# The second MoE product of six token blocks by seven quarter products instead of eight, on one core

## The chip, the cores and the metric

The kernel runs on one core of a Trainium2 chip. The metric is the device time of one launch in microseconds, the median of several runs. A profile of one execution shows what each engine did in it: PE is TensorE (PEld its weight loads), DVE is VectorE, ACT is ScalarE, POOL is GpSimd and SP is SyncE, which issues the DMAs.

## The reference

Retention attention of 8 batches with 8 heads, 576 positions and 64 dimensions, then a gated feed-forward product over all 4608 tokens:

```
scores = scale * q @ k.T                     # per batch and head, 576 x 576
Dmat = gamma_h ** (row - col) where row >= col, else 0
x = (scores * Dmat) @ v                      # heads side by side: 4608 x 512
h = x @ w_in                                 # 512 x 2048
g = h * (1 / (1 + exp(-beta * h)))           # beta per hidden column
out = g @ w_out                              # 2048 x 512, float32
```

## The kernel before

The decay is split into gains for queries and values (`gq`, `gv`), so that attention is linear: the 512 first positions of a batch are worked in chunks, with masked scores inside a chunk (`scores`, L510) and running states between chunks (`fold`, L492), and `outputs4` (L543) adds both parts and leaves `xT`, 512 tokens with the hidden index on the partitions. The last 64 positions of all batches make one more block of 512 tokens (`tail_scores`, `tail_outputs`). There are nine blocks, in the order batch 0 to 6, tails, batch 7.

A block has two products. `up` (L630) is one step of 4 matmuls of 512 columns, for one of 16 groups `fo` of 128 hidden columns; ScalarE's silu (L639) writes the result to `gT`. `down` (L663) makes the output for 128 tokens at a time from 16 matmuls of 512 columns, in steps of 4; `gT` is the stationary side, `w_out_sb` the moving one. The factor 1/beta is in `w_out_sb` (`cast_w_out`, L211), since silu(beta h) is beta times g. VectorE copies each finished `po` to `ot` (L677), and SP stores it.

The order of all engines' instructions is written out by hand. `fill` lists the steps of the products, and `base[n]` is the step at which block n begins. The streams hold pairs of a step number and a piece of other work; `merged` (L690) puts each piece before the step of that number. So one step is 4 matmuls of 512 columns, and a block of 32 steps is followed by the next with no gap. In blocks 2 to 5 the attention of the next batch stands at step 16 (scores and second states) and step 25 or 26 (`outputs4`), in the second product. Loads, the gains on GpSimd (`pre_q` L281, `pre` L318 and L292) and the DMA transposes `x_q`, `x_k` stand a fixed number of steps ahead of the scores that use them (`pair_prep`).

Each engine works its own instructions in that order, and waits by semaphores. Places that the prediction speaks of:

- PSUM tiles take banks by tag: `mm` (3 banks, for `ph`, `po` and the second state bank), `O` (2), `sc` (2), `st` (1). A new tile of a tag waits until the work on the tile whose bank it takes is done.
- `four_states` leaves four state updates in two banks. `fold` adds them one after another in float32 (VectorE, L499, alternately into `sums` and `warm`), and ScalarE copies each sum to a bf16 tile in `sbq` (L503).
[...]
- `load_w_out` brings the four groups of `w_out` in float32 to tiles `wt`, of which there are four.

Of the kernel before, what the change touches and what calls it, by code (L numbers as in the profile page):

```python
# [19 lines left out]
def kernel(  # L20
# [15 lines left out]
    P = 128  # L36
# [11 lines left out]

    blocks = list(range(B - 1)) + [B, B - 1]

    seq = []
# [120 lines left out]
    w_in_sb = wpool.tile([P, KO, d_ff], BF16, name="w_in_sb")  # L172
    w_out_sb = wpool.tile([P, FO, d_model], BF16, name="w_out_sb")
    beta_sb = consts.tile([P, FO], F32, name="beta_sb")
    rbeta_sb = consts.tile([P, FO], F32, name="rbeta_sb")
    tiny = consts.tile([P, FO], F32, name="tiny")
    WG = 4

# [32 lines left out]
    def cast_w_out(g):  # L211
        t = wts.pop(NP + g)
        for i in range(KO):
            fo = g * KO + i
            if g and i == KO - 1:
                nc.scalar.activation(w_out_sb[:, fo, :], t[:, i], ACT.Copy, scale=rbeta_sb[:, fo:fo + 1])
            else:
                nc.vector.tensor_scalar(w_out_sb[:, fo, :], t[:, i], rbeta_sb[:, fo:fo + 1], None, ALU.mult)

    for g in range(NP):  # L220
# [23 lines left out]
    def xt(m):  # L244
        if m not in xts:
            xts[m] = xpool.tile([P, HP, CB, P], BF16, name="xT", tag="xT" if m < B else "xTt", bufs=2 if m < B else 1)
        return xts[m]

    def F(f, *a):
        return lambda: f(*a)  # L250
# [17 lines left out]
    def pre_q(b, n):  # L268

        if n == 0:  # L270
            batch[b] = dict(qs=sb.tile([P, CB, H, D], BF16, name="qs", tag="qs", bufs=2),
                            qT=sb.tile([P, CB, HP, P], BF16, name="qT", tag="qT", bufs=2))
        if b < 2:
            hs, cs = slice(n // 2 * HP, (n // 2 + 1) * HP), slice(n % 2 * 2, n % 2 * 2 + 2)
            e = nc.vector
        else:
            if n % 2:
                return
            cs = slice(n, n + 2)
            for to, hs in turned:  # L280
                nc.gpsimd.tensor_tensor(batch[b]["qs"][:, cs, to], q_tiles[b][:, hs, cs].rearrange("p h i d -> p i h d"),  # L281
                                        gq[:, cs, hs].unsqueeze(3).to_broadcast([P, 2, len(range(H)[hs]), D]), ALU.mult)
            return
        e.tensor_tensor(batch[b]["qs"][:, cs, hs], q_tiles[b][:, hs, cs].rearrange("p h i d -> p i h d"),
                        gq[:, cs, hs].unsqueeze(3).to_broadcast([P, cs.stop - cs.start, hs.stop - hs.start, D]),
                        ALU.mult)

    def pre(i, js=(0, 1)):
# [6 lines left out]
        if b is None:  # L295
# [4 lines left out]
            else:  # L300
                if c == 2:
                    batch[None] = (sb.tile([P, CB, H, D], BF16, name="qs", tag="qs", bufs=2),
                                   sb.tile([P, CB, HP, P], BF16, name="qT", tag="qT", bufs=2))
# [187 lines left out]

    def fold(b, e, bank):  # L492

        for n in range(4):
            new = bank[n // 2][:, n % 2]
# [13 lines left out]

    def scores(b, ccs):  # L510

# [18 lines left out]
        m = late[:].rearrange("k i s -> k (i s)").unsqueeze(1).to_broadcast([P, 2 * HP, TL])  # L530
        for cc in ccs:
            for j in range(2):
                nc.vector.tensor_tensor(R[cc][:, j].rearrange("k n p s -> k (n p) s"),  # L533
                                        sc[cc, j][:].rearrange("k n p s -> k (n p) s"), m, ALU.mult)
        for e in es:
# [6 lines left out]

    def outputs4(b):  # L543

# [29 lines left out]
        paired(*[crosses(j, j) + ahead[j] + crosses(j, 1 - j, None if j else after) for j in range(2)])  # L574
        for n, ((x, y), O) in enumerate(O4.items()):
            to = xt(b)[:, 2 * y:2 * y + 2].rearrange("k p i (c x s) -> k (p i) c x s", c=2, x=2)[:, :, :, x, :]
            (nc.scalar.copy if n == 1 else nc.vector.tensor_copy)(to, O[:].rearrange("k p i (c s) -> k (p i) c s", c=2))  # L577
        if bank:
# [21 lines left out]
    def tail_outputs(i0):  # L600
# [22 lines left out]
        for n, ((x, y), O) in enumerate(O4.items()):  # L623
            to = xt(B)[:, 2 * y:2 * y + 2].rearrange("k p t (x s) -> k (p t) x s", x=2)[:, :, x, :]
            (nc.scalar.copy if n % 2 else nc.vector.tensor_copy)(to, O[:].rearrange("k p t s -> k (p t) s"))

# [3 lines left out]
    def up(m, fo, c0=0, cn=CB):  # L630
        if m not in gts:
            gts[m] = sb.tile([P, FO, CB, P], BF16, name="gT", tag="gT", bufs=2)
        w = slice(c0 * PC, (c0 + cn) * PC)
        ph = psum.tile([P, CB, P], F32, name="ph", tag="mm", bufs=3)
        ph = ph.rearrange("f i s -> f (i s)")[:, :cn * P].rearrange("f (i s) -> f i s", i=CB)
        for ko in range(KO):
            nc.tensor.matmul(ph, w_in_sb[:, ko, fo * P:(fo + 1) * P], xts[m][:, ko, :, w],  # L637
                             start=(ko == 0), stop=(ko == KO - 1))
        nc.scalar.activation(gts[m][:, fo, :, w], ph, ACT.Silu, scale=beta_sb[:, fo:fo + 1])  # L639

    phs = {}

    def ups(m, fs, u, banks):

        if m not in gts:
            gts[m] = sb.tile([P, FO, CB, P], BF16, name="gT", tag="gT", bufs=2)
        if u == 0:
# [15 lines left out]
    def down(m, ms, f0, fn=4, n0=0, nn=d_model):  # L663
# [10 lines left out]
        if ms == 0:  # L674
            ots[m] = stage.tile([P, MB // P, d_model], F32, name="ot", tag="wt", bufs=4)
        ot = ots[m][:, ms, n0:n0 + nn]
# [69 lines left out]
    cast_w_in(1)  # L746
    nc.vector.reciprocal(rbeta_sb[:], beta_sb[:])

    def mask(m, *pattern):
# [25 lines left out]
    for n, m in enumerate(blocks[2:], 2):  # L775
        base[n] = len(fill)
        fill += [F(up, m, fo) for fo in range(FO)]
        subs = range(MB // P) if n < B else range(MB // P - 1)
        fill += [F(down, m, ms, f0) for ms in subs for f0 in range(0, FO, 4)]
    fill += [F(down, blocks[-1], MB // P - 1, 0, FO, n0, nn) for n0, nn in ((0, 256), (256, 128), (384, 128))]  # L780

# [27 lines left out]
    def pair_prep(i, at):  # L809
# [13 lines left out]
        if c == 0:  # L823
# [5 lines left out]
                     (at - 15, F(pre, i + 1)), (at - (13 if c else 11.5), F(x_k, b, c // 2))]  # L829

    todo = list(range(2 * CB, len(seq), 2))
    for n in range(1, B - 1):
# [50 lines left out]
```

## Time and profile before

| | |
|---|---|
| runs, device time | 299.18, 300.15, 301.35 us; median 300.15 |
| profiled execution, span of its instructions | 298.3 us |
| profiled execution, its own time | not given beside the span; the runs lie 0.9 to 3.1 us above it, the median 1.85 |
| TensorE busy | 290.3 us, 97% of the span |
| VectorE, ScalarE, GpSimd busy | 104.8, 142.2, 109.9 us |
| first product, 128x512 matmuls | 480 (L637) and 56 (L652) |
| second product, 128x512 matmuls | 560 (L670) |
| one block from 3 to 5, start to start | 30.4 us |
| the two last blocks | 27.6 us each |

Busy time is time in which the engine had an instruction in work. A row of a group gives the line, engine and operation, what it writes and reads, its shape and count, then busy time and mean length of one instruction, then idle time ahead of such instructions and what ended it. A row of the chain gives the start, the length and the work that the end of the run hung on. Block starts below are read from the chain: 85.02 for batch 2, 115.91 for batch 3, 146.38 for batch 4.

### The profile page before, as it was taken

Reading aid. Unit: us, or ns where it says so; the run is one execution under the profiler, and the core shown is the slowest. Engines: PE = TensorE matmul, PEld = TensorE weight load, DVE = VectorE, ACT = ScalarE, POOL = GpSimd, SP = SyncE. Lnnn points to the kernel's source line nnn. Section 1 sums busy time; section 2 is a strip of 40 time slices with the busy share of each in tenths; the row PEclk is TensorE's granted clock in tenths of the full one; section 3 lists DMA queues with packets and bytes.
Section 4 is the critical chain, followed back from the end, with each engine's and each line's share of the span. In section 5 each row is a group of like instructions: output and inputs, shape, how many; then the busy total and the mean of one; then the engine's idle time right before and its main releaser. Section 6 shows DMA issues by size and latency. Waiting matters only on the chain.

```text
span 298.3 us, 7533 instructions
## 1 busy us (share of the span) xinstructions
PE 290.3 (97%) x3177; PEld 149.3 (50%) x3177; DVE 104.8 (35%) x215; ACT 142.2 (48%) x245; POOL 109.9 (37%) x219
## 2 busy tenths in 40 slices
PE   8799999999899999999999999999999999999995
PEld 5554456855444554455445544454445544444444
DVE  6553556605620564053404450336036600110012
ACT  5577546782238424851485137513752167007600
POOL 4666116763922822292328032863453000000000
PEclk9999999999999999999999999999999999999999
DMA  8999999999999979999893798999989210131012
GB/s 211 219 347 387 385 256 258 208 187 232 193 188 254 297 164 193 253 157 160 229 245 77 158 206 239 192 200 193 199 187 168 74 37 0 35 70 37 0 70 73
DMA packets 128657, 53.98 MB, mean 181 GB/s; under 512 B 110432, under 2 KB 121072, under 8 KB 128624
## 3 DMA queue, kind: packets, MB, share of 16 engines
q1 hardware_dynamic: 128592, 53.49, 78.8%
q8 instruction: 25, 0.41, 0.6%
q14 instruction: 8, 0.07, 0.1%
q10 hardware_dynamic: 32, 0.01, 0.0%
HBM read 36.71 MB, written 9.44 MB: 155 GB/s over the span
## 4 chain that ended last, share of the span: by engine, by line
PE 94%; SPq 2%; DMA 2%; issue 1%; ACT 0%; POOL 0%; DVE 0%
PE po L670 42%; PE ph L637 38%; PE ph L652 4%; PE O L463 3%; DMA kvn<-in_k_dram 2%; SPq L96 2%; PE sc L463 2%; PE st L463 1%; PE O L414 1%; PE sc L367 1%; PE T L348 1%; PE O L400 0%; PE st L436 0%; SPq L82 0%; PE T L342 0%
## 5 line engine op out<-in xcount | busy, mean ns | idle before, releaser
L670 PE MATMUL po<-w_out_sb,gT 128*128 128x512 bf16 (+2 forms) x608 | 128.5, 368 | 0.0
L639 ACT ACTIVATE gT<-ph,beta_sb 128x512 bf16<-128x512 f32 (+1 forms) x140 | 91.4, 657 | 53.7 <-PE ph L637 53.4
L637 PE MATMUL ph<-xT,w_in_sb 128*128 128x512 bf16 (+1 forms) x560 | 114.7, 364 | 0.0
L670 PEld LDWEIGHTS <-gT 128*128 128x128 bf16 x608 | 56.7, 98 | 62.5
L637 PEld LDWEIGHTS <-w_in_sb 128*128 128x128 bf16 x560 | 54.4, 98 | 57.6
L318 POOL CAST kn<-kvn 128x128 bf16<-128x128 f32 (+2 forms) x80 | 25.9, 358 | 54.9 <-DMA kvn<-in_k_dram 54.4
L677 DVE COPY ot<-po 128x512 f32<-128x512 f32 (+2 forms) x34 | 22.4, 657 | 67.2 <-PE po L670 67.2
L533 DVE TENSOR_TENSOR R<-sc,late 128x512 bf16<-128x512 f32 x24 | 15.0, 684 | 67.5 <-PE sc L463 43.7
L292 POOL TENSOR_TENSOR vn<-kvn,gv 128x512 bf16<-128x512 f32 x32 | 33.3, 1042 | 13.1 <-DMA kvn<-in_v_dram 8.4
L281 POOL TENSOR_TENSOR qs<-qn,gq 128x256 bf16<-128x256 f32 (+1 forms) x36 | 26.3, 758 | 26.8 <-DMA qn<-in_q_dram 26.3
L503 ACT CAST sbd<-warm 128x256 bf16<-128x256 f32 x18 | 7.3, 405 | 27.0 <-DVE warm L499 17.6
L577 ACT CAST xT<-O 128x512 bf16<-128x512 f32 x6 | 3.5, 585 | 28.3 <-PE O L463 28.3
L577 DVE CAST xT<-O 128x512 bf16<-128x512 f32 x18 | 11.3, 685 | 4.3 <-PE O L463 4.3
L652 PE MATMUL ph<-xT,w_in_sb 128*128 128x512 bf16 x56 | 12.4, 379 | 0.2 <-ACT xT L424 0.2
L371 DVE TENSOR_TENSOR R<-sc,causal 128x512 bf16<-128x512 f32 x16 | 10.2, 685 | 4.6 <-PE sc L367 4.5
L655 ACT ACTIVATE gT<-ph,beta_sb 128x512 bf16<-128x512 f32 x14 | 8.6, 686 | 4.2 <-PE ph L652 4.2
L201 POOL CAST w_in_sb<-wt 128x256 bf16<-128x256 f32 (+1 forms) x12 | 7.3, 611 | 5.0 <-DMA wt<-in_moe_w_in_dram 4.9
L652 PEld LDWEIGHTS <-w_in_sb 128*128 128x128 bf16 x56 | 5.4, 98 | 6.7 <-issue 0.3
L226 PE MATMUL ph<-warm 128*128 128x128 f32 (+1 forms) x24 | 7.3, 444 | 1.3 <-DVE warm L126 1.3
L503 ACT CAST sbd<-sum 128x256 bf16<-128x256 f32 x18 | 7.3, 405 | 2.0
L499 DVE TENSOR_TENSOR sum<-warm,st 128x256 f32<-128x256 f32 x18 | 7.6, 421 | 1.5
L499 DVE TENSOR_TENSOR warm<-sum,st 128x256 f32<-128x256 f32 x18 | 7.5, 418 | 1.5
(92 smaller groups left out, 160.8 us busy)
## 6 DMA issues: line engine op xcount, KB each, us to landing
qn<-in_q_dram SPq DMA_DIRECT2D x16, 512.0 KB, 5.3
out_dram<-ot SPq DMA_DIRECT2D x31, 256.0 KB, 3.6
kvn<-in_k_dram SPq DMA_DIRECT2D x20, 256.0 KB, 5.1
kvn<-in_v_dram SPq DMA_DIRECT2D x20, 256.0 KB, 5.2
wt<-in_moe_w_out_dram SPq DMA_DIRECT2D x8, 512.0 KB, 9.3
kvn<-in_k_dram SPq DMA_DIRECT2D x24, 128.0 KB, 4.1
kvn<-in_v_dram SPq DMA_DIRECT2D x24, 128.0 KB, 3.7
wt<-in_moe_w_in_dram SPq DMA_DIRECT2D x5, 512.0 KB, 7.8
```

What stands on the lines that cost most here:

```text
L281: nc.gpsimd.tensor_tensor(batch[b]["qs"][:, cs, to], q_tiles[b][:, hs, cs].rearrange("p h i d -> p i h d"), gq[:, cs, hs].unsqueeze(3).to_ ...
L292: nc.gpsimd.tensor_tensor(live[i]["vn"][:], kv_tiles.pop(i)[:, 1], gains(gv, row_of(b, c)), ALU.mult)
L318: nc.gpsimd.tensor_copy(kn[:, c % 2, to], t[:, 0, hs])
L463: ins = nc.tensor.matmul(out, lhsT, rhs, start=start, stop=stop, skip_group_check=True)
L499: nc.vector.tensor_tensor(sums[(e + n + 1) % 2], sums[(e + n) % 2], new, ALU.add)
L533: nc.vector.tensor_tensor(R[cc][:, j].rearrange("k n p s -> k (n p) s"), sc[cc, j][:].rearrange("k n p s -> k (n p) s"), m, ALU.mult)
L577: (nc.scalar.copy if n == 1 else nc.vector.tensor_copy)(to, O[:].rearrange("k p i (c s) -> k (p i) c s", c=2))
L637: nc.tensor.matmul(ph, w_in_sb[:, ko, fo * P:(fo + 1) * P], xts[m][:, ko, :, w], start=(ko == 0), stop=(ko == KO - 1))
L639: nc.scalar.activation(gts[m][:, fo, :, w], ph, ACT.Silu, scale=beta_sb[:, fo:fo + 1])
L652: nc.tensor.matmul(phs[f][:], w_in_sb[:, ko, f * P:(f + 1) * P], xts[m][:, ko], start=(ko == 0), stop=(ko == KO - 1))
L670: nc.tensor.matmul(po[:, :nn], gT[:, fo, ms, :], w_out_sb[:, fo, n0:n0 + nn], start=(fo == 0), stop=(fo == FO - 1))
L677: (nc.scalar.copy if m == 0 else nc.vector.tensor_copy)(ot, po[:, :nn])
```

## The change

In the blocks of batches 3 to 6, the tails and batch 7 the second product is worked by Strassen's scheme. The 512 tokens are cut in two halves (row parts 0, 2 and 1, 3), the 2048 hidden columns in two (even and odd `fo`), the 512 output columns in two. The eight quarter products become seven, each of sums of quarters, and VectorE and ScalarE combine them to the four output quarters. Each of the seven is 16 matmuls of 256 columns: 8 hidden groups for two row parts.

- The weight sums (`b7`) are built once, in the block of batch 2, from the float32 `wt` tiles that `cast_w_out` now leaves in place: ScalarE scales them with 1/beta of the even group, VectorE makes five of the seven, GpSimd two. Groups 1 to 3 take `wt` tiles as these come free. Because even and odd groups share one scale, `up` writes the odd groups' silu to a float32 tile `hs`, and VectorE multiplies by `ratio` into `gT`.
- The sums of `gT` (`sa`) are made by VectorE in each block: products 3 and 4 need none, products 1, 5 and 2 half sums in two parts, 7 and 6 whole ones.
- The products run in the order 3, 4, 1, 5, 2, 7, 6 in three PSUM chains U (3, 2, 6), W (4, 5), Z (1, 7), tag `mm`; in the last block each chain has a bank for each row part.
- The scores of batch 4 move from step 16 to step 8 of the block ahead, those of batches 5 to 7 to step 5, `outputs4` to step 15, the tail's scores from 24.7 to 18.5 and its outputs from 28.5 to 24; their loads, gains and transposes move with them by 8 to 11 steps. Masks and folds are handed out one by one between the steps (`later`). Batches 4 to 7 copy `sbq` on VectorE, and ScalarE copies all four outputs.
- `gT` and `qs` have one tile instead of two, `xT` of the tails shares the tag of the others, `ot` has a tag of its own.

```diff
+    def scale_w_out(g, i):
+        f = g * KO + i - i % 2
+        t = wts[NP + g]
+        nc.scalar.activation(t[:, i], t[:, i], ACT.Copy, scale=rbeta_sb[:, f:f + 1])
+    def seven_b(g, j):
...
+        t = wts[NP + g]
+        b11, b12, b21, b22 = (t[:, r::2, c * NH:(c + 1) * NH] for r in range(2) for c in range(2))
+        to = sevens[g][:, j - 1]
+        if j in (2, 5):
+            nc.vector.tensor_scalar(to, b11 if j == 2 else b22, -1.0, None, ALU.mult)
+            return
+        x, y, op = {1: (b11, b22, ALU.add), 3: (b12, b22, ALU.subtract), 4: (b21, b11, ALU.subtract),
+                    6: (b11, b12, ALU.add), 7: (b21, b22, ALU.add)}[j]
+        (nc.gpsimd if j > 5 else nc.vector).tensor_tensor(to, x, y, op)
...
-            nc.scalar.copy(sbq[e + n], sums[(e + n + 1) % 2])
+            (nc.vector.tensor_copy if b > SB else nc.scalar.copy)(sbq[e + n], sums[(e + n + 1) % 2])
...
+        if m >= SB and fo % 2:
+            h = scratch[0][:, fo // 2 % 4].rearrange("f (i s) -> f i s", i=CB)
+            nc.scalar.activation(h, ph, ACT.Silu, scale=beta_sb[:, fo:fo + 1])
+            nc.vector.tensor_scalar(gts[m][:, fo], h, ratio[:, fo // 2:fo // 2 + 1], None, ALU.mult)
+            return
...
+    def seven_a(m, j, ks=slice(0, KH)):
+        x, y, op = {1: ((0, 0), (1, 1), ALU.add), 5: ((0, 0), (1, 0), ALU.add), 2: ((0, 1), (1, 1), ALU.add),
+                    7: ((1, 0), (1, 1), ALU.subtract), 6: ((0, 1), (0, 0), ALU.subtract)}[j]
+        nc.vector.tensor_tensor(sums_a[0][:, held_in[j], ks], quarter(m, *x, ks), quarter(m, *y, ks), op)
+    chain_of = {3: "U", 2: "U", 6: "U", 4: "W", 5: "W", 1: "Z", 7: "Z"}
+    def seven_mm(m, j, p, alone):
...
+        for k in range(KH):
+            if j in (3, 4):
+                a = gts[m][:, 2 * k + (j == 4), 2 * p + (j == 4), :]
+            else:
+                a = sums_a[0][:, held_in[j], k, p, :]
+            nc.tensor.matmul(chains[c, n][:, 0 if alone else p], a, sevens[k // 2][:, j - 1, k % 2, :],
+                             start=j in (3, 4, 1) and k == 0 and (alone or p == 0), stop=k == KH - 1, skip_group_check=True)
+        if alone or p == 1:
+            seven_out(m, j, slice(p, p + 1) if alone else slice(0, 2), n)
+    def seven_out(m, j, ps, n):
...
+        if j == 4:
+            nc.scalar.copy(c12, W[:])
+            nc.vector.tensor_tensor(c21, c12, U[:], ALU.add)
+        elif j == 1:
+            nc.scalar.copy(c22, Z[:])
+        elif j == 5:
+            nc.scalar.copy(c11, W[:])
+            nc.vector.tensor_tensor(c12, c21, c11, ALU.subtract)
+        elif j == 2:
+            nc.vector.tensor_tensor(c21, c21, U[:], ALU.subtract)
+        elif j == 7:
+            nc.vector.tensor_tensor(c11, c11, Z[:], ALU.add)
+            seven_store(m, 0, ps)
+        elif j == 6:
+            nc.vector.tensor_tensor(c22, c22, U[:], ALU.add)
+            seven_store(m, 1, ps)
...
+            fill += [F(seven_mm, m, j, p, n == B) for j in seven for p in range(2)]
...
+    for g in range(WG):
+        t = base[2] - 15 + 3.5 * g
+        streams.append([(t + 0.7 * x, F(scale_w_out, g, x)) for x in range(KO)])
+        t = base[2] + 1.2 + 3.5 * g
+        streams.append([(t + 0.45 * x, F(seven_b, g, j)) for x, j in enumerate((3, 4, 1, 5, 2, 7, 6))] +
+                       [(t + 3.2, F(last_seven, g))])
...
+        early = {3: 13, 4: 11, 5: 11, 6: 11}.get(n, 9)
+        streams.append([(t + early + 0.6 * x, F(seven_a, m, j, first)) for x, j in enumerate((1, 5, 2))] +
+                       [(t + 16.1, F(seven_a, m, 1, second)), (t + 16.2, F(seven_a, m, 5, second)), (t + 18, F(seven_a, m, 2, second)),
+                        (t + 20, F(seven_a, m, 7)), (t + 22, F(seven_a, m, 6))])
...
-        at = [t + 17, base[b] - 9.5] if n == 1 else [t + 3, t + 18] if n < B - 2 else [t + 3, t + 10, t + 17, t + 24]
+        sh = {1: 0, 2: 0, 3: 8}.get(n, 11)
+        at = [t + 17, base[b] - 9.5] if n == 1 else [t + 3 - sh, t + 18 - sh] if n < B - 2 else [t - 7, t, t + 9, t + 16]
...
-        elif n < B - 2:
-            streams.append([(t + 16, F(group1, b, (0, 1))), (t + 25, F(outputs4, b))])
         else:
-            streams.append([(t + 16, F(group1, b, (0, 1))), (t + 21.5, F(outputs4, b)),
-                            (t + 24.7, F(tail_scores, take[2])), (t + 28.5, F(tail_outputs, take[2]))])
+            t0 = t + (8 if n == 3 else 5)
+            rest, outs = [], []
+            streams.append([(t0, F(scores, b, (0, 1), rest))] + queued(span(t0 + 0.1, 4, 0.9) + span(t0 + 3.7, 4, 0.7), rest))
+            streams.append([(t + 15, F(outputs4, b, outs))] + queued([t + 16.3] * 4, outs))
+            if n < B - 2:
+                streams.append(queued(span(t + 17.5, 4, 0.6), outs))
+            else:
+                streams.append([(t + 18.5, F(tail_scores, take[2])), (t + 24, F(tail_outputs, take[2]))])
```

More of the change, by code (lines that the diff above doesn't have):

```diff
@@ L49 @@
     blocks = list(range(B - 1)) + [B, B - 1]
+    SB = 3
+    KH = FO // 2
+    NH = d_model // 2
+    seven = (3, 4, 1, 5, 2, 7, 6)
     seq = []
@@ L490, in four_states, with fold @@
                 for x in range(2)]
-    def fold(b, e, bank):
-        for n in range(4):
+    def fold(b, e, bank, ns=range(4)):
+        for n in ns:
             new = bank[n // 2][:, n % 2]
@@ L530, in scores @@
         m = late[:].rearrange("k i s -> k (i s)").unsqueeze(1).to_broadcast([P, 2 * HP, TL])
[L531 to L534, printed above, removed]
+        masked = [F(nc.vector.tensor_tensor, R[cc][:, j].rearrange("k n p s -> k (n p) s"),
+                    sc[cc, j][:].rearrange("k n p s -> k (n p) s"), m, ALU.mult) for cc in ccs for j in range(2)]
+        if later is not None:
+            later += masked + [F(fold, b, e, bank, (n,)) for e in es for n in range(4)]
+            return
+        for f in masked:
+            f()
         for e in es:
@@ L541, in new_O4, with outputs4 @@
         return live[lead]["O4"]
-    def outputs4(b):
+    def outputs4(b, later=None):
         i0 = b * CB
@@ L574, in outputs4, with out @@
         paired(*[crosses(j, j) + ahead[j] + crosses(j, 1 - j, None if j else after) for j in range(2)])
-        for n, ((x, y), O) in enumerate(O4.items()):
+        def out(n, x, y, O):
             to = xt(b)[:, 2 * y:2 * y + 2].rearrange("k p i (c x s) -> k (p i) c x s", c=2, x=2)[:, :, :, x, :]
-            (nc.scalar.copy if n == 1 else nc.vector.tensor_copy)(to, O[:].rearrange("k p i (c s) -> k (p i) c s", c=2))
+            e = nc.scalar.copy if n == 1 or later is not None else nc.vector.tensor_copy
+            e(to, O[:].rearrange("k p i (c s) -> k (p i) c s", c=2))
+        outs = [F(out, n, x, y, O) for n, ((x, y), O) in enumerate(O4.items())]
+        if later is not None:
+            later += outs + ([F(fold, b + 1, 0, bank, (n,)) for n in range(4)] if bank else [])
+            return
+        for f in outs:
+            f()
         if bank:
```

70 lines of the change are left out of this document (56 added, 14 removed).

## The prediction

> **What bounds the kernel now.** First the page's busy line, slices and chain by line, then the chain in order of time, then groups kept apart by shape, then waits and queues around the places that the change touches.
>
> ```profile
> PE 290.3 (97%) x3177; PEld 149.3 (50%) x3177; DVE 104.8 (35%) x215; ACT 142.2 (48%) x245; POOL 109.9 (37%) x219
> PEclk9999999999999999999999999999999999999999
> PE 94%; SPq 2%; DMA 2%; issue 1%; ACT 0%; POOL 0%; DVE 0%
> ...
> 239.66 13.81 PE ph L637 x64
> 253.47 13.81 PE po L670 x64
> ```
>
> TensorE is busy for 97% of the span at full clock, and 94% of the chain is TensorE alone: whatever stops it lengthens the run, and only TensorE work taken away shortens it. A block's second product is 64 matmuls in 13.81 us, 216 ns each. VectorE is busy for 35%.
>
> ```profile
> 53.44 1.31 PE ph L637 x12
> ...
> L637 PE MATMUL ph<-xT,w_in_sb 128*128 128x256 bf16 x80 | 9.7, 273 | 0.0
> L637 PEld LDWEIGHTS <-w_in_sb 128*128 128x128 bf16 x560 | 54.4, 98 | 57.6
> ```
>
> These twelve have 256 columns and load new weights each: 1.31 / 12 = 109 ns. The 98 ns weight load still hides, so a half-width matmul costs half.
>
> ```profile
> L533 DVE TENSOR_TENSOR R<-sc,late 128x512 bf16<-128x512 f32 x24 | 15.0, 684 | 67.5 <-PE sc L463 43.7 <-PE ph L637 13.5 <-issue 10.2
> L218 DVE TENSOR_SCALAR w_out_sb<-wt,rbeta_sb 128x512 bf16<-128x512 f32 x13 | 5.9, 485 | 5.4 <-DMA wt<-in_moe_w_out_dram 5.4
> L499 DVE TENSOR_TENSOR warm<-sum,st 128x256 f32<-128x256 f32 x18 | 7.5, 418 | 1.5
> L203 DVE CAST w_in_sb<-wt 128x256 bf16<-128x256 f32 x8 | 2.5, 318 | 2.9 <-DMA wt<-in_moe_w_in_dram 2.9
> L343 DVE COPY qT<-T 128x1024 bf16<-128x1024 bf16 x2 | 1.4, 692 | 1.3 <-PE T L342 1.3
> L577 ACT CAST xT<-O 128x512 bf16<-128x512 f32 x6 | 3.5, 585 | 28.3 <-PE O L463 28.3
> ```
>
> These are the prices (mean ns of one, after the busy time) of the vector and scalar work that the change adds.
>
> **The change, part by part.**
>
> *Matmuls.* 64 of 512 columns become 7 x 16 = 112 of 256: 112 x 108 ns = 12.1 us against 13.81, 1.7 less in each of six blocks: **-10.2 us**. Nothing else leaves TensorE.
>
> *Added vector work per block.* Eight multiplications of hs (row L218, 0.485), the sums of gT, and five combinations of the output (0.684, row L533) instead of four 0.69 copies; for batches 4 to 7 the seven sbq copies (0.318, row L203) also come from ScalarE. A half sum has 1024 two-byte elements from SBUF, both operands. No row is that. Nearest by type is L343, 1024 two-byte elements in 0.69; nearest by operation is f32, 0.684 for 512 and 0.418 for 256, which is 1.04 ns an element and 1.21 for 1024. I take 0.69 (1.22 for a whole sum by the same slope) and keep 1.21 (2.3) as the upper end. [...] Per block this is 22 us of VectorE against some 10 now, in 29 us. The mean fits. What counts is where TensorE waits for the end of this in-order queue. Four masks in a row took 2.48 us, so an instruction that waits for nothing starts 0.08 before its forerunner ends; my queue times use that.
>
> *Wait 1, the bank of Z (blocks of batches 3, 4, 5).* Product 1 (Z) gets the PSUM bank that held the next batch's second pair of states. So it waits for the fold's last read of that bank, and the vector queue holds this read behind c21, which waits for the ScalarE copy of W, thus for the end of product 4. Count from the end of fo 15's matmuls. TensorE is through products 3 and 4 at 3.45. VectorE starts at 0.8 (silu 0.69 and two handovers) with one multiplication 0.485, three half sums 2.07, four fold steps 1.68, three copies 0.95, c21 0.68: 5.9 us, 5.5 with the overlaps. It ends at 6.3: **a wait of 2.9 us, three times 8.6**. Were the queue empty, what stays is the copy of W 0.585, c21 0.684, one fold 0.42 and handovers 0.2: 1.9, three times 5.7. With sums at 1.21 it is 4.5, three times 13.4. Even the lowest takes all that a block saved.
>
> *Wait 2, the fence in outputs4.* Its memset stands in the same queue, and half of the state products wait for it. Block of batch 4, from its first up: five ups 4.3, scores and states 1.0, ten ups 8.6, first part of outputs4 1.3: TensorE is there at 15.2. On VectorE everything after fo 5's multiplication (7.0) is back to back: five multiplications, four masks, four folds, three copies, three half sums, 9.9 summed, 8.7 overlapped: fence at 15.7. About **0.55** for batches 4 and 5 (none to 2.2), **0.9** in the block of batch 6. In the block of batch 3 two masks stand behind fo 9's multiplication, whose silu ends only at 10.3; the last sbq copy is 1.0 late and the fence 1.2 more: **2.2** (0.7 to 3.8). The tail fence behind the whole queue, and a scalar copy ahead of the tail scores, add **0.65** (to 4.3).
>
> *Wait 3, building the seven weight sums in the block of batch 2.* From the timelines and the chain, each row with its start and length:
>
> ```profile
> 90.95 1.04 POOL L292 TENSOR_TENSOR vn<-kvn,gv 128x512 bf16<-128x512 f32 x1 [0.48 <-DMA kvn<-in_v_dram]
> 97.69 1.04 POOL L281 TENSOR_TENSOR qs<-qn,gq 128x512 bf16<-128x512 f32 x1 [5.70 <-DMA qn<-in_q_dram]
> ...
> 91.89 1.15 SPq L82 DMA_DIRECT2D qn<-in_q_dram  x2
> ...
> 102.57 0.43 PE st L463 x32
> ```
>
> Four groups of five vector and two GpSimd instructions alternate; a group's buffer comes free only when both engines are through with the group before. GpSimd has batch 3's keys until 92.0 (first row, its end), then b7 group 0 until 94.0, one of group 1 until 95.0. Then batch 4's qs stands in the same queue: its load moves from 91.9 to about 90.1, behind the four stores that SP issues until 90.05, and lands 5.8 later as now: 96.0. Its first half takes 2.2 (98.2), the rest of group 1 to 99.2, the other half to 101.4, group 2 to 103.4. Only then may VectorE do group 3 (2.7, to 106.1), and behind it stands the fold of batch 3's first states, two steps to 107.0. The second states need that bank at 102.57: **a wait of 4.5 us** (2 to 6, as the load lands). Now this fold starts at 99.31.
>
> *The rest.* The 8 x 0.585 us that ScalarE gets in outputs4 lie under the products; sixteen in-place scalings (0.72 each) lie in the block of batch 1, where ScalarE idles. The end: now a 0.29 copy and a 64 KB store (landing 1.8); then a 0.42 addition and 256 KB (3.6, from the issues' median under load): **+1.6** (0.3 to 2.2). Earlier loads: kT of batch 4 must land for scores eight steps (6.9 us) sooner. SP now idles from 102.4 to 107.3 behind a store, batch 4's last keys had 4.7 us to spare, and wait 3 gives time back: nothing taken, up to 3.
>
> Sum: -10.2 + 8.6 + (2.2 + 1.1 + 0.9 + 0.65) + 4.5 + 1.6 = **+9.4**. The page's span is 298.3, the runs' median 300.15, so 1.85 lies around it: 298.3 + 9.4 + 1.85 = 309.5. The low ends give -10.2 + 5.7 + 0.7 + 0.65 + 2 + 0.3 = -0.9 (299.3); the high ends +29 (329).
>
> **The rivals.**
>
> *The vector queue is never late* (not slower). Place: Z's wait. If VectorE is ready for c21 when W's copy is, 1.9 a block stays, and b7's building is nearly hidden: the low ends, 299.3. It decides once the 5.5 us between fo 15's silu and the fold drops below 4.5 and group 3 ends by 101. For it: 65% idle VectorE now. Against: every price above is a row, and 5.5 is the sum of twelve instructions.
>
> *Sums at one element a cycle*: waits 1 and 2 at their upper ends with 4.5 in the block of batch 2: about 325. For it: both f32 rows. Against: L343.
>
> *The clock falls after the long wait.* The longest gap inside the dense part is now 1.1 us, at full clock, so nothing shows what 4.5 us do. If the array then ran at half speed for as long as the gap, half of 4.5 is lost: 311.8. [...]
>
> *Keys late*: scores of batches 4 to 7 wait 1 us each for kT: 313.5. For it: DMA share 0.8 to 1.16 from 85 to 207 us. Against: loads move as far as the scores.
>
> *It saves no TensorE time*, should 256 columns with gT as weights cost over 123 ns: 320. The 109 ns row speaks against it.
>
> **How the numbers follow.** My forecast, slower by the three waits: 0.60. Queue never late: 0.19, of which 0.08 with still less than the floors. One element a cycle 0.07, clock 0.07, keys 0.05, no saving 0.02. A measurement here tells about 1% from no change: faster means under 297.1, slower over 303.2. Faster is that 0.08; within 1% are the other 0.11 of the first rival and 0.04 of the forecast, with half its waits: 0.15; slower 0.77. The range for 8 in 10 goes from 299, the low ends, to 318, halfway to the one-element case.
>
> **What would show it.** Right: matmuls of the seven products at 108 ns; TensorE waits of 2 to 3 us ahead of Z in three blocks, put down to VectorE's fold; under 1 us at the fence in the blocks of batches 4 and 5; one wait near 103 us of 4 to 5 us for the fold of batch 3; the two last blocks dense, at 25.9 us each. Half sums at 0.69. Wrong: no TensorE idle ahead of Z, half sums at 1.2, a granted clock under 0.9 after 103 us, or scores waiting for a transpose.

## The result and the profile after

The changed kernel takes 331.06 us (median of 4 runs, 327.49 to 333.49) against 299.98 beside it: the ratio is 1.095, 95% interval 1.089 to 1.101. Medians here are of all runs; ratios and intervals leave out executions more than 1.5% above the quickest of their kernel, and the traces of two runs below, the early building (331.54 us) and the repairs without held loads (314.60 us), are of such executions. The prediction, 309.5 in a range of 299 to 318, had the direction and the three places right, and was far too low. The profiled execution has a span of 327.5 us, 29.2 more than before. First its page: the busy line, the granted clock in 40 slices, the chain by engine.

```profile
PE 288.9 (88%) x3405; PEld 178.6 (55%) x3433; DVE 193.0 (59%) x355; ACT 158.3 (48%) x272; POOL 134.9 (41%) x227
PEclk9999999999999599999799969997999999999999
PE 60%; DVE 19%; DMA 8%; SPq 7%; issue 2%; ACT 2%; POOL 1%; DVEq 0%; POOLq 0%
```

TensorE's share of the chain fell from 94% to 60%; VectorE, no part of it before, has 19%. And the clock, full throughout before, has four slices below. TensorE's waits (for which tile, for whom; us in total, times, longest):

```profile
PE Z L721 <- DVE sum L536: 10.0, 3, 4.1
PE st L500 <- DVE sum L536: 8.1, 1, 8.1
PE O L500 <- DVE fenced L506: 5.7, 5, 1.9
PE sc L500 <- DMA kT<-kn: 3.5, 2, 2.0
...
PE O L500 <- DVE sbq L540: 0.6, 1, 0.6
```

The first three are the waits 1, 3 and 2 of the prediction, the fourth is its rival of the late keys (`kT`, the transposed keys). The seven products themselves do what was counted: in the chain each takes 1.75 us for 16 matmuls wherever nothing waits, so 12.25 a block against 13.81, and the two last blocks last 26.05 us each (forecast 25.9, before 27.63 and 27.8).

How the Z wait comes about, in the block of batch 4: VectorE's timeline (start, length, instruction), then TensorE's. `sa` are the half sums, `ot<-ot,U` is the prediction's c21, the addition of U to the copy of W for one output quarter (second half of the tokens, first of the columns).

```profile
185.30 0.49 DVE L691 TENSOR_SCALAR gT<-hs,ratio 128x512 bf16<-128x512 f32 x1 [2.25 <-ACT hs L690]
185.82 1.29 DVE L705 TENSOR_TENSOR sa<-gT 128x1024 bf16<-128x1024 bf16 x2
...
189.40 0.68 DVE L540 CAST sbd<-sum 128x256 bf16<-128x256 f32 x1
...
190.66 0.69 DVE L735 TENSOR_TENSOR ot<-ot,U 128x512 f32<-128x512 f32 x1
191.26 0.42 DVE L536 TENSOR_TENSOR sum<-warm,st 128x256 f32<-128x256 f32 x1
```
```profile
186.12 1.91 PE L721 MATMUL W<-b,gT 128*128 128x256 bf16 x16
191.74 3.60 PE L721 MATMUL Z<-b,sa 128*128 128x256 bf16 x16 [3.70 <-DVE sum L536]
```

VectorE first idles 2.25 us for ScalarE, then works without a gap until the last addition of the second state bank ends at 191.68, and Z starts at 191.74. That is the prediction's queue, 6.4 us here against 5.5 worked out. What the prediction did not have is in the last line: 16 matmuls take 3.60 us in place of 1.75. The granted clock is 0.50 from 192 to 196, behind the wait.

The wait at the state bank, in the block of batch 2 (VectorE, then TensorE): the bank's last reader ends at 112.05, forecast 107.0.

```profile
111.63 0.42 DVE L536 TENSOR_TENSOR sum<-warm,st 128x256 f32<-128x256 f32 x1
...
112.19 0.65 PE L500 MATMUL st<-vn,kn 64*64 64x64 bf16 x32 [8.10 <-DVE sum L536]
```

The clock fell in or behind four waits in this trace: this one (0.50 from 106 to 112), the Z waits of 4.06 and 3.70 us, and a wait of 1.92 us for the fence in the block of batch 5 (0.50 to 0.52 from 221 to 224). It stayed full (1.00) behind the third Z wait (2.22 us) and behind the longer wait for keys (2.01 us).

### The profile page after: what moved, and what is told of

It reads as the page before. It is cut to its first block, busy times and chain, and to the rows that moved or that the text cites. A ratio compares the mean times of both kernels' runs of the same rounds, so it can differ in the third digit from the quotient of the medians.

```text
span 327.5 us, 8212 instructions
## 1 busy us (share of the span) xinstructions
PE 288.9 (88%) x3405; PEld 178.6 (55%) x3433; DVE 193.0 (59%) x355; ACT 158.3 (48%) x272; POOL 134.9 (41%) x227
## 4 chain that ended last, share of the span: by engine, by line
PE 60%; DVE 19%; DMA 8%; SPq 7%; issue 2%; ACT 2%; POOL 1%; DVEq 0%; POOLq 0%
PE ph L686 23%; PE po L788 11%; PE U L721 8%; PE Z L721 7%; DVE sa L705 4%; PE W L721 4%; SPq L100 3%; DVE gT L691 2%; DMA wt<-in_moe_w_in_dram 2%; DMA qn<-in_q_dram 2%; PE ph L770 2%; DVE sbd L540 2%; PE O L500 2%; DVE b L248 2%; DVE R L287 2%
## 5 line engine op out<-in xcount | busy, mean ns | idle before, releaser
L693 ACT ACTIVATE gT<-ph,beta_sb 128x512 bf16<-128x512 f32 (+1 forms) x92 | 58.4, 641 | 51.1 <-PE ph L686 46.1
L721 PEld LDWEIGHTS <-sa 128*128 128x128 bf16 x480 | 48.8, 102 | 18.3 <-DVE sum L536 10.8
L691 DVE TENSOR_SCALAR gT<-hs,ratio 128x512 bf16<-128x512 f32 x48 | 26.6, 555 | 50.2 <-ACT hs L690 50.0
L690 ACT ACTIVATE hs<-ph,beta_sb 128x512 f32<-128x512 f32 x48 | 33.0, 687 | 26.7 <-PE ph L686 25.6
L788 PE MATMUL po<-w_out_sb,gT 128*128 128x512 bf16 x184 | 43.2, 386 | 1.1 <-issue 1.0
L705 DVE TENSOR_TENSOR sa<-gT 128x1024 bf16<-128x1024 bf16 (+1 forms) x48 | 41.5, 895 | 4.5 <-PE Z L721 4.2
L721 PE MATMUL Z<-b,sa 128*128 128x256 bf16 x192 | 26.3, 297 | 10.0 <-DVE sum L536 10.0
L788 PEld LDWEIGHTS <-gT 128*128 128x128 bf16 x192 | 18.4, 99 | 21.6 <-issue 1.3
L721 PE MATMUL U<-b,sa 128*128 128x256 bf16 x192 | 22.9, 273 | 0.0
L287 DVE TENSOR_TENSOR R<-sc,late 128x512 bf16<-128x512 f32 x24 | 15.3, 682 | 12.4 <-issue 10.2
L721 PEld LDWEIGHTS <-gT 128*128 128x128 bf16 x192 | 19.1, 100 | 4.1 <-issue 0.5
L248 DVE TENSOR_TENSOR b<-wt 128x512 bf16<-128x512 f32 x12 | 11.3, 998 | 7.4 <-POOL b L248 7.3
L408 DVE TENSOR_TENSOR R<-sc,causal 128x512 bf16<-128x512 f32 x16 | 10.2, 685 | 4.6 <-PE sc L404 4.5
L721 PE MATMUL W<-b,sa 128*128 128x256 bf16 x96 | 12.5, 288 | 0.0
```

The source lines that it names most:

```text
L690: nc.scalar.activation(h, ph, ACT.Silu, scale=beta_sb[:, fo:fo + 1])
L691: nc.vector.tensor_scalar(gts[m][:, fo], h, ratio[:, fo // 2:fo // 2 + 1], None, ALU.mult)
L705: nc.vector.tensor_tensor(sums_a[0][:, held_in[j], ks], quarter(m, *x, ks), quarter(m, *y, ks), op)
L721: nc.tensor.matmul(chains[c, n][:, 0 if alone else p], a, sevens[k // 2][:, j - 1, k % 2, :], start=j in (3, 4, 1) and k == 0 and (alone o ...
L788: nc.tensor.matmul(po[:, :nn], gT[:, fo, ms, :], w_out_sb[:, fo, n0:n0 + nn], start=(fo == 0), stop=(fo == FO - 1))
```

## The experiments

**The clock behind a pause.** 14 pauses of chosen length in the kernel before:

```diff
...
+        if m in gaps and fo in (4, 12):
+            for _ in range(gaps[m][fo // 12]):
+                nc.vector.tensor_copy(idle[:], past[0][:].rearrange("f i s -> f (i s)"))
+            nc.tensor.matmul(ph[:, 0, :TL], idle[:, :P], idle[:, :TL], start=True, stop=True)
+        past[0] = ph
```

> The kernel before with 14 pauses of TensorE put into the up projections of batches 2 to 7 and the tails: at each, VectorE copies a bank 2 to 10 times (some 0.69 us each as the mask from PSUM takes, so pauses of about 1.5 to 7 us, 77 copies and about 57 us in all), then TensorE goes on. Nothing else is changed. Theory C (the clock is halved behind a pause over some length near 3 us): short pauses (2 to 4 copies) leave the following matmuls at 216 ns, the long ones are followed by some 3.5 us at half speed, about 1.7 us lost each, so 300 + 57 + 9 times 1.7 = 372. Theory N (the slow matmuls in the changed kernel come from their operands, not from the wait): 357, every matmul behind a pause as quick as before it.

Measured 389.0 (two runs, one of them traced). The pauses are 2.23 to 8.03 us, 66.8 in all. The matmul that ends a pause, in TensorE's timeline (the pause is in brackets):

```profile
90.33 0.20 PE L640 MATMUL ph<-idle 128*128 128x64 bf16 x1 [2.23 <-DVE idle L639]
188.88 0.20 PE L640 MATMUL ph<-idle 128*128 128x64 bf16 x1 [3.68 <-DVE idle L639]
322.51 0.23 PE L640 MATMUL ph<-idle 128*128 128x64 bf16 x1 [7.31 <-DVE idle L639]
```

and the 1.5 us stretches behind these three (length, TensorE's busy time and instructions, granted clock, DMA share, GB/s):

```profile
90.53:92.03 1.50, 1.50 (x8) 0.86 1.04 380
92.03:93.53 1.50, 1.50 (x5) 0.50 1.22 225
93.53:95.03 1.50, 1.50 (x5) 0.50 1.01 315
95.03:96.53 1.50, 1.50 (x8) 1.00 1.08 362
...
189.08:190.58 1.50, 1.50 (x8) 1.00 0.00 0
...
322.71:324.21 1.50, 1.50 (x5) 0.50 0.02 5
324.21:325.71 1.50, 1.50 (x5) 0.50 0.00 0
325.71:327.21 1.50, 1.50 (x6) 0.52 0.00 0
327.21:328.71 1.50, 1.50 (x9) 1.00 0.00 0
```

Added up over such stretches, the clock is at half for 3.0 to 4.8 us behind 12 of the 14 pauses; behind one of 2.96 and one of 3.68 it stays full. TensorE's busy time is 315.6 (the span of 389.5 less 70.6 of listed waits and, as before, 3.3 at the end) against 290.3; 14 small matmuls make 3.1 of the 25.3, so a drop costs about 22.2 / 12 = 1.85 us, with no trend in the length of the pause. Theory C is right that the pause halves the clock, and wrong in its threshold near 3 us, which lies between the Z waits of 2.22 (clock full behind it) and 3.70 us (half): 2.23 is enough here (1.92 in the changed kernel), and 3.68 need not be. The length alone does not decide it: pauses of 2.96 and of 3.68 us each came twice, once with a drop and once without. What else decides was not shown.

**The order in VectorE's queue.** First the additions of the states are set closer together, so that the last one goes ahead of c21:

```diff
-                streams.append(queued(span(t + 17.5, 4, 0.6), outs))
+                streams.append(queued(span(t + 17.5, 4, 0.45), outs))
```

> The changed kernel with one thing moved: the last addition of the second state bank is issued ahead of the addition for c21 (blocks of batches 3, 4 and 5), so that the bank which product 1 waits for comes free earlier. Theory Q (the length of VectorE's queue ahead of that addition sets the wait): each of the three Z waits (4.1, 3.7, 2.2 us) is shorter by one c21, 0.69 us, so 2.1 us in all, to about 329. Theory C (on top of that TensorE's clock is halved for some 3.5 us behind a wait over about 3 us, which is what 8.8 us of the added busy time are): where a wait falls under that length the 16 matmuls behind it take 1.75 instead of 3.6 us as well, up to 1.8 us for each of two blocks, so 325 to 329. Theory R (the bank is released by something else, c21 only stood beside it): 331, no change.

Measured 330.96, ratio 1.102 (1.096 to 1.108): nothing gained. The wait in the block of batch 3 went from 4.06 to 3.44, as asked, but that in the block of batch 4 from 3.70 to 4.57, and all three together from 10.0 to 10.7. There c21 did leave the queue, and two half sums took 2.43 us in place of 1.29 and a copy of `sbq` 1.18, with GpSimd at work. Inconclusive by itself; it shows that the queue's length is not fixed by its list. Then all four additions go ahead of the last scaling multiply, into the 2.25 us that VectorE idles:

```diff
-            streams.append([(t + 15, F(outputs4, b, outs))] + queued([t + 16.3] * 4, outs))
-            if n < B - 2:
-                streams.append(queued(span(t + 17.5, 4, 0.6), outs))
+            streams.append([(t + 15, F(outputs4, b, outs))])
+            if n < B - 2:
+                streams.append([(t + 15, lambda outs=outs: outs.pop(4)())] * 4)
+            streams.append(queued([t + 16.3] * 4, outs))
...
```

> The changed kernel with the four additions of the first states issued right behind attention's outputs, ahead of the last scaling multiply and of the second half sums, in the blocks of batches 3, 4 and 5. In the changed kernel VectorE idles 2.24 us there for ScalarE while the banks are already full. Theory Q (the order of VectorE's queue makes the Z waits): the banks are free before W ends, the three waits (10.0 us) fall under 2 us in all and the half clock behind two of them (3.6 us) goes, so 331 becomes 318 to 321. Theory V (VectorE has simply too much work in these 8 us, whatever the order): the second half sums come as much later as the additions come earlier, product 1 then waits for sums in place of its bank, 328 or more.

Measured 317.64, ratio 1.058 (1.054 to 1.062), and TensorE's list of waits is:

```profile
PE st L500 <- DVE sum L536: 7.4, 1, 7.4
PE O L500 <- DVE fenced L506: 6.5, 5, 1.9
PE sc L500 <- DMA kT<-kn: 3.6, 2, 2.6
```

No Z wait is left. The same instructions in another order are some 11 us faster by the two ratios: theory Q holds, theory V falls.

**VectorE beside GpSimd.** Rows of the changed kernel by stretch (line, instruction, shapes, count, busy us, mean ns): the building of weight groups 1 to 3 on VectorE and GpSimd, then VectorE in the blocks of batches 3 to 5, and in the last two blocks, where GpSimd idles.

```profile
L248 DVE TENSOR_TENSOR b<-wt 128x512 bf16<-128x512 f32 x9 | 9.5, 1103 | 7.4 <-POOL b L248 7.3
L244 DVE TENSOR_SCALAR b<-wt 128x512 bf16<-128x512 f32 x6 | 6.3, 1084 | 0.0
...
L248 POOL TENSOR_TENSOR b<-wt 128x512 bf16<-128x512 f32 x6 | 8.8, 1484 | 0.1
...
L691 DVE TENSOR_SCALAR gT<-hs,ratio 128x512 bf16<-128x512 f32 x24 | 14.2, 591 | 25.6 <-ACT hs L690 25.5
L705 DVE TENSOR_TENSOR sa<-gT 128x1024 bf16<-128x1024 bf16 x18 | 13.9, 794 | 0.1
...
L691 DVE TENSOR_SCALAR gT<-hs,ratio 128x512 bf16<-128x512 f32 x16 | 7.8, 487 | 17.0 <-ACT hs L690 16.9
L705 DVE TENSOR_TENSOR sa<-gT 128x1024 bf16<-128x1024 bf16 x12 | 7.8, 687 | 0.1
```

To see whether GpSimd is the cause, it was loaded in the last two blocks with work that nothing waits for, in a kernel that works the seven products in these two blocks alone and builds the weight sums on VectorE (the one that comes out faster below):

```diff
...
+    streams.append([(base[7] + 0.4 * x, F(nc.gpsimd.memset, load[:], 1.0)) for x in range(70)])
+    streams.append([(base[8] + 0.6 * x, F(nc.gpsimd.tensor_tensor, made[:], load[:], load[:], ALU.mult)) for x in range(42)])
```

> The kernel with the spread build, and GpSimd, which has nothing to do in the last two blocks, loaded there with work that nothing waits for: 70 memsets of 128x256 f32 in the block of the tails, 42 multiplies of two SBUF operands (128x256) in the block of batch 7. With GpSimd idle VectorE's rows there are 687 ns for a half sum (two bf16 operands from SBUF), 1219 for a whole one, 487 for the scaling multiply (f32 from SBUF to bf16) and 686 for 128x512 f32 with one operand from PSUM. [...] Theory D (the long rows in the changed kernel come from DMA traffic or from VectorE's own queue, not from GpSimd): all rows keep their times to 5%, since there is no more DMA traffic in these blocks than before. The time should be within 2 us of the kernel without the load under either, as VectorE has slack there.

Time 299.39 in one run. The same two groups, under the memsets (first two lines) and under the multiplies:

```profile
L690 DVE TENSOR_SCALAR gT<-hs,ratio 128x512 bf16<-128x512 f32 x8 | 3.9, 486 | 8.5 <-ACT hs L689 8.5
L706 DVE TENSOR_TENSOR sa<-gT 128x1024 bf16<-128x1024 bf16 x6 | 3.9, 687 | 0.1
...
L706 DVE TENSOR_TENSOR sa<-gT 128x1024 bf16<-128x1024 bf16 x6 | 6.1, 1058 | 0.1
L690 DVE TENSOR_SCALAR gT<-hs,ratio 128x512 bf16<-128x512 f32 x8 | 5.6, 698 | 5.8 <-ACT hs L689 5.7
```

Nothing under memsets (486 and 687 ns, 487 and 687 with GpSimd idle); 54% and 43% longer under multiplies of two SBUF operands (1058 and 698 ns), while additions with an operand from PSUM kept 408 to 421 ns for 256 columns (422 with GpSimd idle). Theory D falls: it is GpSimd's work that makes these rows long, the multiplies and not the memsets. The half sum reads two tensors from SBUF, the scaling multiply one, and both got longer; by what means GpSimd holds them up no run here shows.

**Building the weight sums earlier.** VectorE alone makes all seven, groups 0 and 1 in the block of batch 1:

```diff
-        (nc.gpsimd if j > 5 else nc.vector).tensor_tensor(to, x, y, op)
+        nc.vector.tensor_tensor(to, x, y, op)
...
-    for g in range(WG):
-        t = base[2] - 15 + 3.5 * g
...
-        t = base[2] + 1.2 + 3.5 * g
...
+    for g, (t, u) in enumerate(((-36, -27), (-31, -20), (-14, 1), (-7, 7.5))):
+        streams.append([(base[2] + t + 0.9 * x, F(scale_w_out, g, x)) for x in range(KO)])
+        streams.append([(base[2] + u + 0.8 * x, F(seven_b, g, j)) for x, j in enumerate((3, 4, 1, 5, 2, 7, 6))] +
...
```

> The changed kernel with the tables built by VectorE alone and in other places: groups 0 and 1 in the second half of the block of batch 1 (where VectorE was busy 1.4 us of 10), 2 and 3 in the first half of the block of batch 2. Theory B (the build, two engines taking turns, made the 8.1 us wait at the state bank and with the clock behind it some 2 more): that wait is gone, 331 becomes 320 to 322. Theory L (the build only kept VectorE busy, and what is late is the state's other input): the wait at the state bank in the block of batch 2 stays at 5 us or more and the time at 326 or more.

Measured 328.12, ratio 1.081 (1.078 to 1.085). The wait at the state bank is gone, as theory B said, but by the two ratios only some 4 us are gained, where theory B had 9 to 11. In the execution traced, other waits are longer:

```profile
PE Z L721 <- DVE sum L536: 12.1, 3, 5.1
PE O L500 <- DVE fenced L506: 6.9, 5, 1.9
PE sc L500 <- DMA kT<-kn: 6.4, 2, 4.5
```

TensorE waits 4.49 us for keys at batch 4's scores, 2.01 in the changed kernel. How much of this the other executions had is not shown.

**The move without the products.** `SB` is the first block that works the seven products; here no block reaches it, and the streams that build the weight sums are taken out:

```diff
-    SB = 3
+    SB = 9
...
-    for g in range(WG):
-        t = base[2] - 15 + 3.5 * g
...
```

> The changed kernel without the seven products: all blocks use the second product as before, none of the tables for it are built, and the attention of batches 4 to 7 stays in the first half of the block ahead (the rows of the tail block come out in another order, since its columns are laid down for the products). Theory P (the products with their build and sums are what costs, the move is nearly free): the waits for the fence (5.7 us in five in the changed kernel, of which the kernel before has some too) and for late keys (3.5) are the only ones left, so 300 to 305. Theory M (the move itself is what costs, since the state banks, the fence and the keys all come earlier than their engines can serve them): 312 or more, with waits at the state banks of 2 us or more in each block.

Measured 307.91, ratio 1.028 (1.021 to 1.035): by the ratios 8.4 us of the change's 28.5 are the move's, between the two theories. (With the move this kernel keeps the single tiles of `gT` and `qs` and the output copies on ScalarE, so these are in the 8.4 too; the copies of `sbq` are back on ScalarE.) TensorE has two waits over 1 us that the kernel before lacks, 2.40 for batch 3's keys at 104.46, with a clock of 0.81 and 0.97 in the 8 us stretches from 100 and 108, and 1.48 in `outputs4`. SyncE's queue shows why the keys are late; in the kernel before it holds

```profile
90.50 1.34 SPq L326 DMA_TRANSPOSE kT<-kn  x1
91.89 1.15 SPq L82 DMA_DIRECT2D qn<-in_q_dram  x2
```

and with the move

```profile
89.69 1.86 SPq L86 DMA_DIRECT2D qn<-in_q_dram  x2
...
94.70 4.90 SPq L105 DMA_DIRECT2D kvn<-in_k_dram  x2
...
101.06 1.28 SPq L363 DMA_TRANSPOSE kT<-kn  x1
```

GpSimd finished these keys at 90.5 before and at 90.3 with the move, but the next batch's loads, eight steps earlier now, stand ahead of the transpose, which leaves 10.6 us later. The prediction compared loads with the scores of their own batch, and not with the batch ahead in the queue.

**The fence on another engine.**

```diff
-        f = nc.vector.memset(fenced[:], 0.0)
+        f = nc.scalar.copy(fenced[:, :1], lscale[:])
```

> The changed kernel with its fence (the small write that TensorE waits for between two groups of matmuls into one bank) on ScalarE in place of VectorE. In the changed kernel five fences are waited for, 5.7 us in all, 0.8 to 1.9 each, and VectorE had a scaling multiply or half sums in hand each time. Theory Q (the wait is the rest of what VectorE has in its queue): ScalarE has done with its last projection there, so each wait becomes some 0.4 us or less, 3.7 us in all less, and 331 becomes 326.5 to 328. Theory F (the wait is the way there and back between the engines, whichever it is): 330 or more.

Measured 327.40, ratio 1.091 (1.088 to 1.095). The five waits of 5.7 us became one of 0.6 us: theory Q for the wait. Of the time the interval cannot say (it overlaps that of the change), and the Z waits rose to 11.3.

**All repairs together**, without and with the loads held back behind the transposes (`load_q` and `load_kv` of batches 4 to 7 by 8, 6, 6 and 6 steps):

```diff
+        ld = {4: 8, 5: 6, 6: 6, 7: 6}.get(b, 0)
...
-            st += [(at - 30, F(load_q, b, (0,)))] + ([(at - 30, F(x_k, XB, 1))] if b == XB + 1 else [])
+            st += [(at - 30 + ld, F(load_q, b, (0,)))] + ([(at - 30, F(x_k, XB, 1))] if b == XB + 1 else [])
...
```

> The changed kernel with three of its waits taken away at once: additions of the first states ahead of the sums (317.6 by itself), tables built earlier and by VectorE alone, fence on ScalarE. The loads and the transposes of the keys stay in the order of the changed kernel. Theory S (the waits add up: Z bank 10.0, state bank 8.1, fence 5.7, with the slow clock behind the long ones): 331 - 13.5 - 8 - 2 - 4 = 303 to 305. Theory K (keys that are late behind loads on SyncE's queue take the place of what is taken away, as in the run with the early build, where that wait grew from 3.5 to 6.4 us): 307 to 311, with waits for keys of 5 us or more.

Measured 309.87, ratio 1.032 (1.028 to 1.036), the size that theory K gave; in the execution traced, TensorE waits 7.2 us for keys, and 5.4 us for `gT` ahead of W.

> The same, and the loads for batches 4 to 7 are issued 6 to 8 steps later, so that on SyncE's queue each transpose of keys stands ahead of the next batch's loads again, as before the change. Theory K (the queue's order makes the keys late): no wait for keys over 1 us, 4 us or more less than without this, 299 to 303. Theory D (the transposes take longer because more is moved at that time): keys are as late as without this, same time to 1 us; and if the loads themselves are now late, GpSimd's casts are, with new waits for keys.

Measured 305.44, ratio 1.020 (1.015 to 1.025), no wait for `kT` over 1 us, and a new one:

```profile
PE st L500 <- POOL vn L329: 5.6, 2, 4.7
PE W L721 <- DVE gT L691: 1.5, 2, 1.0
```

So the order made the keys late, as theory K says, but its 299 to 303 was missed: held back, the loads make `vn`, GpSimd's scaled values, late for batch 4, as the end of theory D says. By the ratios 3.6 us are gained. TensorE is busy for 282.8 us, 7.5 less than before; the idle time still eats it.

**Where the products stand alone.** Only the tails and batch 7, attention at its old steps, the weight sums built with GpSimd in the blocks of batches 5 and 6:

```diff
-    SB = 3
+    SB = 7
...
-        t = base[2] + 1.2 + 3.5 * g
+        t = base[5] + 12 + 8 * g
```

> Seven products for the tail block and batch 7 alone, where no attention is left to work; attention at its old steps, the build of the tables spread over the blocks of batches 5 and 6. In the changed kernel these two blocks last 26.05 us each against 27.63 and 27.8 before. Theory P (the products gain what their matmuls say wherever VectorE and GpSimd are free): 3.3 us less there, at most 1 us given back by the build and the end, so 296.5 to 298, faster than both. Theory R (the build with GpSimd in step slows VectorE wherever it is put, and attention of batches 6 and 7 with it): the blocks of batches 5 and 6 get longer by 3 us or more and the time is 300 or above.

Measured 300.81, ratio 1.002 (0.999 to 1.005): nothing gained. One copy of a finished `po` out of PSUM stood on VectorE behind five building instructions, three of them 1.36 us each beside GpSimd:

```profile
205.73 4.08 DVE L248 TENSOR_TENSOR b<-wt 128x512 bf16<-128x512 f32 x3
209.74 0.75 DVE L244 TENSOR_SCALAR b<-wt 128x512 bf16<-128x512 f32 x2
210.41 0.68 DVE L796 COPY ot<-po 128x512 f32<-128x512 f32 x1
```
```profile
211.14 13.93 PE L685 MATMUL ph<-xT,w_in_sb 128*128 128x512 bf16 x56 [2.04 <-DVE ot L796]
```

The clock was 0.83 from 210 to 220. So VectorE alone builds them, one group in the nearly idle first half of each of four blocks:

```diff
-        (nc.gpsimd if j > 5 else nc.vector).tensor_tensor(to, x, y, op)
+        nc.vector.tensor_tensor(to, x, y, op)
-        t = base[5] + 12 + 8 * g
...
+        streams.append([(base[3 + g] + 1 + 1.6 * x, F(seven_b, g, j)) for x, j in enumerate((3, 4, 1, 5, 2, 7, 6))] +
+                       [(base[3 + g] + 12, F(last_seven, g))])
```

> Seven products for the tails and batch 7 alone, as in the run with both last blocks, but the tables are built by VectorE alone, one group of four rows in the first half of each of the blocks of batches 3 to 6, where VectorE of the kernel before has next to nothing to do (0.0 to 0.65 us busy in 10). In the run before this one the build, in step with GpSimd in the blocks of batches 5 and 6, made one eviction late: TensorE waited 2.04 us at 211.1 and its clock was 0.83 in the 10 us behind that. Theory W (that one wait, with the clock behind it, ate the gain): it goes, 2.0 us of waiting and 1.8 to 2.1 of slow clock, so 300.8 becomes 296.5 to 297.5, some 1% faster than before. Theory R (the build costs wherever it lies, since VectorE and ScalarE then lack the time for attention): 299.5 or more, with a new wait.

Measured 297.60 against 299.88, **ratio 0.993 (0.991 to 0.995)**, faster than both kernels, and just above what was expected. The wait is gone from the trace and the granted clock is 0.999 over its span, as theory W has it. By the two ratios 2.5 us came back, and the edit moves the whole building, so that the share of this one wait is not told apart from the rest; the clock fell only in some executions of the run before (three of its twelve ran at full clock throughout, at 299.65 to 301.14 us). With the block of batch 6 as a third (`SB = 6`, batch 7's attention moved into it):

> Seven products for the last three blocks (batch 6, tails, batch 7), the attention of batch 7 and the tails in the block of batch 6 as in the changed kernel, that of the others at its old steps, fence on ScalarE, tables built by VectorE alone in the first halves of four blocks, loads of batch 7 held back. With the last two alone and that build it is 297.6. Theory P (a block gains its 1.7 us if nothing in it is late): 296 to 297. Theory M (attention and products in one block keep VectorE and ScalarE too busy, as in the changed kernel where the block of batch 6 took 32.9 us against 32.4 before): 298 or more.

Measured 302.10, ratio 1.008 (1.005 to 1.011), runs from 299.52 to 304.29: theory M's number, but the trace, of the quickest run, shows one wait of 2.48 us for batch 7's `qT` (its transposed queries) and no other over 1 in the dense part. Which wait makes the other runs longer was not traced.

## Why the prediction was wrong in size, step by step

It is taken against the span: +9.4 forecast, +29.2 measured.

| step of the sum | forecast | measured |
|---|---|---|
| matmuls | -10.2 | -9.4 (6 x (13.81 - 12.25)) |
| wait 1, bank of Z | 8.6 | 10.0 |
| wait 2, fence and `sbq` | 4.85 | 6.3 |
| wait 3, state bank in the block of batch 2 | 4.5 | 8.1 |
| end | 1.6 | 0.7 (4.0 from TensorE's last matmul to the end, before 3.3) |
| keys | 0 | 3.5 |
| half clock behind waits | 0 | 8.0 (busy 288.9 against 290.3 - 9.4) |
| small waits, as what is left | 0 | 2.0 |

*Matmuls, wait 1, wait 2*: right in mechanism and place, and in the sums nearly in size. That the fold behind c21 sets Z, and the vector queue the fence, is shown by the runs that reordered the one and moved the other to ScalarE. Half sums cost 687 ns, as priced, in the two last blocks, where GpSimd idles. The upper end of 1.21 us, an estimate from f32 rows and called one element a cycle in the chances, was not their mean in any block: beside GpSimd, in the blocks of batches 3 to 5, it is 794 ns. Block by block it is rougher, and the sums came near in part by luck: the Z waits are 4.06, 3.70 and 2.22 us for three times 2.9, and the fence in the block of batch 5 took 1.92 for 0.55. The *end* cost less than half of what was forecast.

*Wait 3* was mis-sized by the price of the building instructions. "Group 3 ends 106.1, fold 107.0" used 0.485 and 0.684; the rows beside GpSimd are 1084 and 1103 ns, and GpSimd's own 1.48 us in place of 1.04. The bank's last reader ended at 112.05, 5.0 us later than forecast, and TensorE came there 1.5 us later, behind a wait for keys. The prediction let the engines alternate and let them hand over buffers, but priced each as if alone.

*The clock* is the largest miss. It stood as a rival with 0.07, for the one wait of 4.5 us, and at nothing in the sum. The made pauses cost 1.85 us of half clock behind 12 of 14, from 2.2 us up. In the changed kernel the clock fell in or behind four waits, of 8.1, 4.06, 3.70 and 1.92 us: two of them Z waits, which the sum has at 2.9 with no clock behind them. Four times 1.85 is 7.4 of the 8.0.

*Keys late* was a rival with 0.05 and came true beside the forecast: the rivals were held to exclude one another, and the clock, the keys and the longer wait 3 are all in the result. The range shut out their sum. Two of the prediction's own signs of being wrong came: a clock under 0.9 (0.75 from 100 to 110), and scores that wait for a transpose. Why the keys are late, loads ahead of their transpose on SyncE's queue, is shown by the move alone (2.40 us) and by the run that holds the loads back; the prediction held against it that loads move as far as their own scores.

## What to carry to other kernels

A wait of TensorE of about 2 us or more cost its own length here and, behind 12 of 14 made pauses and four waits of the changed kernel, about 1.85 us more by the half clock; with TensorE 97% busy, count both before weighing a matmul saving against it. Price VectorE's instructions with SBUF operands by rows in which GpSimd works beside them (half sums 794 ns for 687, scaling multiplies 591 for 487 in the blocks of batches 3 to 5), and when a load is moved forward, list what on the same queue it now overtakes. A saving goes first where the engines that pay for it are idle: two blocks of the change gain 0.7%, six cost 9.5%.

## What the runs showed of the hardware

- The clock dropped after 12 of 14 pauses put into dense matmuls (`gaps`), the shortest 2.23 us, and did not after one of 2.96 and one of 3.68; the half clock then lasted 3.0 to 4.8 us, with no trend in the length of the pause. In the changed kernel it dropped after a wait of 1.92 us, and not after 2.01 and 2.22.
- GpSimd's multiplies of two SBUF operands lengthened a bf16 half sum on VectorE from 687 to 1058 ns and a scaling multiply from 487 to 698 (`pool_load`); under its memsets they took 687 and 486.
